# Sliding-window attention with SwiGLU and a top-2 mixture: host layouts replace the transposes of q and k

## The chip, the cores and the metric

The kernel runs on one core of a Trainium2 chip. The metric is the device time of one execution in microseconds (us). Inputs are laid out on the host before the launch, and that is not part of the time.

## The reference

Three stages follow one another. First, attention over 4 batches, 8 heads, 576 positions and 64 channels, in which a position sees itself and the 63 before it. Second, an RMS norm and a SwiGLU layer on 2304 tokens of 512, whose weights arrive as float64. Third, a noisy top-2 mixture of 8 experts.

```python
scores = scale * np.matmul(q, k.transpose(0, 1, 3, 2))
mask = (rel >= 0) & (rel < window)          # window = 64
attn = np.exp(scores - max) / (sum + 1e-09)
x = np.matmul(attn, v)                      # then (B * S, H * D)
xn = x / rms * rms_g
x = (silu(xn @ w_gate) * (xn @ w_val)) @ w_out
...
out[mask] += top2_w[mask, k, None] * (np.maximum(x[mask] @ w1[e], 0.0) @ w2[e])
```

## The kernel before

**Attention.** Work comes in 48 tasks: a task `n` is 192 positions (three windows of 64) of two heads. Task `n` belongs to group `rb = n // 4` of positions and head pair `hp = n % 4`; three groups make a batch. The functions, in the order of a task, are these. `load_qk` and `load_v` issue the DMAs on SP's queue, for two tasks at a time (index `m`), from q, k and v as they lie in memory, in runs of 64 floats. `att_t` (L199) transposes q and k on PE, four transposes into one PSUM bank (L207); DVE copies one head's q into the tile `qz` with the factor -0.125 (L213), ACT the other's (L215), and ACT copies k into `kT` (L224), a tile that holds a zero window and all 576 positions of a head pair. `qz` has two buffers and holds, for each of the three windows, a 128 by 128 block whose two diagonal quarters are the two heads and whose other quarters are zero. `att_s` (L228) multiplies them (L233, tile `sc`), adds the mask and takes the minimum on DVE (L238), takes exp on ACT (L241) and divides on POOL (L245). `att_p` transposes the result (L252, tile `pp`, ACT copy to `pT` in L254), and `att_v` multiplies with v (L268, tile `pv`, ACT copy to `xT` in L272).

**SwiGLU.** Tokens come in 6 blocks of 384 (`NB`), two groups of attention to a block. The hidden layer comes in 12 chunks of 128 (`NF`); a step `s` is one chunk of one block. `norm_a` to `norm_c` norm a block and split it into a high and a low float32r part (`xnH`, `xnL`), `m1_half` (L398, tile `gv`) and `m1_out` (L431, tile `x`) are the matmuls, three per product. The weights of a chunk `fc` are three pages (`raw`), loaded once in block 0 by `load_w` (L334); `conv_a` (ACT, L349 and L350) and `conv_b` (DVE and POOL, L361 to L364) turn float64 bits into float32, `split_w` (L369) splits them. There are 24 pages in all.

**Order.** The first eight tasks run ahead of block 0. Eight more run in each of the blocks 0 to 4, for the next block, spread over its steps by `plan_att`: the slots `at(i, ...)` are emptied between the parts of the steps. A scheduler then sets the order on each engine from this order of code. Each queue works in order. All loads named here share SP's queue. `RT`, `LG`, `AO` and their like are tables of slot numbers that don't change. The experts follow after block 5 and don't change either.

Of the kernel before, what the change touches and what calls it, by code (L numbers as in the profile page):

```python
# [23 lines left out]
def tile_window_attention_swiglu_top2(  # L24
# [139 lines left out]
    def rows(src, m, lo, ap):  # L164
        rb, hq = divmod(m, H // NH)
        b, g = divmod(rb, GS)
        o = ((b * H + NH * hq) * S + g * RG + lo) * D
        return bass.AP(tensor=src.tensor, offset=src.offset + o, ap=ap)

    qs, ks, vs, kTs, kw = {}, {}, {}, {}, {}  # L170

    def load_qk(m):
        for src, name, tiles_ in ((q, "qs", qs), (k, "ks", ks)):
            t = attn.tile([RG // 2, 2, NH, D], F32, name=f"{name}{m}", tag=name, bufs=2)
            for c in range(2):
                nc.sync.dma_start(t[:, c], rows(src, m, c * RG // 2, [[D, RG // 2], [S * D, NH], [1, D]]))
            tiles_[m] = t

    def load_v(m):
        w = attn.tile([P, 3, NH, D], F32, name=f"vw{m}", tag="vw", bufs=NVW)  # L180
        vs[m] = w
        first = (m // (H // NH)) % GS == 0
        if first:
            nc.gpsimd.memset(w[0:64, 0], 0.0)
        if m < VD:
            for i in range(3):
                nc.sync.dma_start(w[64:128, i], rows(v, m, i * WIN, [[D, WIN], [S * D, NH], [1, D]]))
            if not first:
                VE(w[0:64, 0], vs[m - H // NH][64:128, 2])
            VE(w[0:64, 1:3], w[64:128, 0:2])  # L190
            return
        if first:
            nc.sync.dma_start(w[64:128, 0], rows(v, m, 0, [[D, WIN], [S * D, NH], [1, D]]))
# [2 lines left out]
        for i in range(1, 3):
            nc.sync.dma_start(w[:, i], rows(v, m, (i - 1) * WIN, [[D, P], [S * D, NH], [1, D]]))

    def att_t(n):  # L199
        rb, hp = divmod(n, HP)  # L200
        m, u = divmod(n, 2)
        hs = slice(2 * u, 2 * u + 2)
        pt = bank(f"pt{n}")
        for i, a in enumerate((qs[m], ks[m])):
            for c in range(2):
                o = i * RG + c * RG // 2
                nc.tensor.transpose(pt[:, o:o + RG // 2], a[:, c, hs].rearrange("p h d -> p (h d)"),  # L207
                                    ident[:RG // 2, :RG // 2])
        for h in range(2):
            s = slice(64 * h, 64 * h + 64)  # L210
            sv = pt[s, :RG].rearrange("d (i c) -> d i c", c=64)
            if h == 0:
# [933 lines left out]
```

## Time and profile before

| | us |
|---|---|
| median of 3 runs | 1109.2 |
| lowest and highest of them | 1109.14, 1111.27 |
| the profiled execution | 1112.73 |
| its span in the trace | 1111.0 |
| PE busy in it | 1053.1 |
| DVE busy | 621.7 |
| ACT busy | 552.5 |
| POOL busy | 435.3 |

The span runs from the first to the last instruction of the profiled execution; its own time is 1.7 us longer, since it takes in what lies around the span. Busy time is the time in which an engine works on an instruction. Matmuls overlap, and their ends are modelled, so the distance between the starts of two PE rows tells more than their lengths. A row of the timeline is a start, a length, an engine, a line of the kernel, an operation, the tile written and the tiles read, the shape and a count (several like instructions in a row are one row), and in brackets how long the engine stood idle before and what ended that.

### The profile page before, as it was taken

Reading aid. Unit: us, or ns where it says so; the run is one execution under the profiler, and the core shown is the slowest. Engines: PE = TensorE matmul, PEld = TensorE weight load, DVE = VectorE, ACT = ScalarE, POOL = GpSimd, SP = SyncE. Lnnn points to the kernel's source line nnn. Section 1 sums busy time; section 2 is a strip of 40 time slices with the busy share of each in tenths; the row PEclk is TensorE's granted clock in tenths of the full one; section 3 lists DMA queues with packets and bytes.
Section 4 is the critical chain, followed back from the end, with each engine's and each line's share of the span. In section 5 each row is a group of like instructions: output and inputs, shape, how many; then the busy total and the mean of one; then the engine's idle time right before and its main releaser. Section 6 shows DMA issues by size and latency. Waiting matters only on the chain. (4 is left out here: it accounts for less than half of the span.)

```text
span 1111.0 us, 17699 instructions
## 1 busy us (share of the span) xinstructions
PE 1053.1 (95%) x6452; PEld 938.5 (84%) x6452; DVE 621.7 (56%) x1638; ACT 552.5 (50%) x1265; POOL 435.3 (39%) x456
## 2 busy tenths in 40 slices
PE   7688889999999999999999999999999999999993
PEld 6577778889889898988989888898989898989882
DVE  4899996766565565657576752433425343435420
ACT  6768766656565665556553522433334343433420
POOL 4366662352244225224523326334334344443211
PEclk9799999999999999999999999999999999999997
DMA  8846427111120121100020406544445445455311
GB/s 179 243 137 208 144 71 252 40 44 43 30 55 13 57 45 44 43 16 1 2 67 20 142 12 170 140 127 86 139 95 148 95 141 100 138 112 144 74 16 26
DMA packets 116408, 101.64 MB, mean 91 GB/s; under 512 B 82048, under 2 KB 94576, under 8 KB 116320
## 3 DMA queue, kind: packets, MB, share of 16 engines
q0 software_dynamic: 17904, 49.07, 18.1%
q1 hardware_dynamic: 98416, 51.42, 16.6%
q8 instruction: 52, 0.85, 0.3%
q14 instruction: 36, 0.29, 0.1%
HBM read 80.55 MB, written 19.92 MB: 90 GB/s over the span
## 5 line engine op out<-in xcount | busy, mean ns | idle before, releaser
L398 PE MATMUL gv<-xnH,gvH 128*128 128x384 f32 x576 | 203.9, 355 | 4.2 <-ACT xnH L325 3.2
L889 PE MATMUL y<-wH,hh 128*128 128x512 f32 (+1 forms) x608 | 202.3, 399 | 0.0
L398 PE MATMUL gv<-xnH,gvL 128*128 128x384 f32 x576 | 196.2, 342 | 4.3 <-DVE gvL L375 4.3
L398 PE MATMUL gv<-xnL,gvH 128*128 128x384 f32 x576 | 196.2, 341 | 0.0
L431 PE MATMUL x<-woHL,hh 128*128 128x512 f32 x648 | 174.5, 404 | 5.0 <-ACT hh L416 4.1
L384 POOL TENSOR_TENSOR woHL<-wo,woHL 128x512 fp32r<-128x512 f32 x72 | 99.3, 1380 | 147.2 <-ACT woHL L383 147.1
L431 PEld LDWEIGHTS x<-woHL,hh 128*128 128x128 f32 x648 | 119.1, 190 | 28.0 <-ACT hh L416 4.9
L889 PEld LDWEIGHTS y<-wH,hh 128*128 128x128 f32 (+1 forms) x608 | 112.9, 186 | 29.9 <-issue 1.0
L600 DVE TENSOR_TENSOR wL<-st,wH 128x1024 fp32r<-128x1024 f32 x64 | 78.3, 1227 | 100.0 <-ACT wH L599 97.9
L713 PE MATMUL h<-xpl,wH 128*128 128x272 f32 (+3 forms) x448 | 133.5, 298 | 0.2 <-issue 0.2
L713 PE MATMUL h<-xph,wH 128*128 128x272 f32 (+3 forms) x448 | 133.3, 298 | 0.0
L713 PE MATMUL h<-xph,wL 128*128 128x272 f32 (+3 forms) x448 | 133.3, 298 | 0.0
L911 POOL DMA_INDIRECT out_dram<-ys,tid x38 | 59.5, 1566 | 186.6 <-ACT ys L904 141.1
L723 DVE SCALAR_TENSOR_TENSOR hh<-h,hh 128x272 fp32r<-128x272 f32 (+6 forms) x232 | 69.6, 325 | 105.8 <-ACT hh L719 89.9
L889 PE MATMUL y<-wL,hh 128*128 128x512 f32 (+2 forms) x328 | 128.4, 395 | 0.1
L719 ACT ACTIVATE hh<-h 128x160 fp32r<-128x160 f32 (+4 forms) x184 | 61.7, 344 | 133.0 <-PE h L713 94.7
L398 PEld LDWEIGHTS gv<-xnH,gvH 128*128 128x128 f32 x576 | 109.3, 190 | 7.8 <-ACT xnH L325 4.0
L398 PEld LDWEIGHTS gv<-xnH,gvL 128*128 128x128 f32 x576 | 109.3, 190 | 6.2 <-DVE gvL L375 5.7
L398 PEld LDWEIGHTS gv<-xnL,gvH 128*128 128x128 f32 x576 | 109.4, 190 | 0.9
L375 DVE TENSOR_TENSOR gvL<-gv,gvH 128x1024 fp32r<-128x1024 f32 (+1 forms) x73 | 92.0, 1262 | 14.4 <-ACT gvH L372 12.1
L245 POOL TENSOR_TENSOR pm<-pm,st 128x384 f32<-128x384 f32 x48 | 41.1, 856 | 133.8 <-DVE st L244 97.0
L372 ACT ACTIVATE gvH<-gv 128x1024 fp32r<-128x1024 f32 x72 | 75.7, 1051 | 21.9 <-PE gv L398 15.0
(208 smaller groups left out, 1924.7 us busy)
## 6 DMA issues: line engine op xcount, KB each, us to landing
vw<-in_v_dram SPq DMA_DIRECT2D x60, 128.0 KB, 3.0
raw<-in_moe_w_gate_dram SPq DMA_DIRECT2D x12, 512.0 KB, 7.5
raw<-in_moe_w_val_dram SPq DMA_DIRECT2D x12, 512.0 KB, 4.4
raw<-in_moe_w_out_dram SPq DMA_DIRECT2D x12, 512.0 KB, 4.5
out_dram<-zero SPq DMA_DIRECT2D x1, 4864.0 KB
qs<-in_q_dram SPq DMA_DIRECT2D x48, 96.0 KB, 2.6
ks<-in_k_dram SPq DMA_DIRECT2D x48, 96.0 KB, 2.6
x2d<-xs SPq DMA_DIRECT2D x18, 256.0 KB, 2.0
```

The source lines that it names most:

```text
L245: nc.gpsimd.tensor_tensor(p, p, st[:, :, 3:4].to_broadcast([P, 3, P]), op=ALU.mult)
L372: nc.scalar.activation(h, gv[fc], AF.Copy)
L375: eng.tensor_tensor(l[:, f], gv[fc][:, f], h[:, f].bitcast(F32), op=ALU.subtract)
L384: nc.gpsimd.tensor_tensor(o[:, 512:], wo[fc], o[:, :512].bitcast(F32), op=ALU.subtract)
L398: nc.tensor.matmul(ps, a, b, start=n == 0, stop=n == 3 * KD - 1)
L431: nc.tensor.matmul(X2[j][t], a, b, start=fc == 0 and n == 0, stop=fc == NF - 1 and n == 2)
L600: nc.vector.tensor_tensor(lo, a, ho.bitcast(F32), op=ALU.subtract)
L713: nc.tensor.matmul(ps, w, x, start=i == 0, stop=i == 3 * KD - 1)
L719: nc.scalar.activation(hh[:, c0 - p0:c1 - p0], ps[:, c0 - lo:c1 - lo], AF.Relu)
L723: nc.vector.scalar_tensor_tensor(hh[:, l.start + a - s.start:l.start + b - s.start], ps[:, a + p0 - lo:b + p0 - lo], 0.0, hh[:, a:b].bitca ...
L889: nc.tensor.matmul(ps[:a.shape[1]], a, b, start=i == 0, stop=i == len(terms) - 1)
L911: nc.gpsimd.indirect_dma_start(out=out, out_offset=bass.IndirectOffsetOnAxis(ap=r[:m], axis=0), in_=y[:m], in_offset=None, compute_op=ALU. ...
```

## The change

On the host, q is laid out as one block of 128 (two heads by 64 channels) by 192 for each task, the 192 in the order position within the window, then window; k as 128 by 576 for each batch and head pair; v as positions by heads by channels, so that four heads of a position are one run of 256 floats. The float64 weights are laid out as pages of 128 by 512, as they are wanted in memory.

In the kernel `att_t` is gone. `load_q` loads each head of a task straight into its half of `qz`, which is now 128 by 2 by 192 with the other half zeroed once, in six buffers. `load_k` loads k straight into `kT`, 192 positions first and the other 384 with the second group. Both are issued four tasks ahead. The scores' stationary operand for window `i` is every third column of `qz`, from `i` on. The factor -0.125 moves into the masking instruction on DVE, and the mask's constant is scaled to suit.

```diff
+FAR = -8.0 * MASKED
...
-    NQ = 2
+    NQ = 6
...
-    qz = [attn.tile([P, 3, P], F32, name=f"qz{i}") for i in range(NQ)]
-    for t in qz:
-        nc.gpsimd.memset(t[0:64, :, 64:128], 0.0)
-        nc.gpsimd.memset(t[64:128, :, 0:64], 0.0)
+
+    qz = [attn.tile([P, 2, RG], F32, name=f"qz{i}") for i in range(NQ)]
...
+    def load_q(n):
+        rb, hp = divmod(n, HP)
+        for h in range(2):
+            d = slice(64 * h, 64 * h + 64)
+            nc.sync.dma_start(qz[n % NQ][d, h], q[rb, hp, d])
+            if n < NQ:
+                (nc.vector if n == 0 else nc.gpsimd).memset(qz[n][d, 1 - h], 0.0)
+
+    def load_k(n):
+        rb, hp = divmod(n, HP)
         b, g = divmod(rb, GS)
...
+        if g == 0:
+            kTs[hp] = attn.tile([P, WIN + S], F32, name=f"kT{n}", tag="kT", bufs=NKT)
+            nc.gpsimd.memset(kTs[hp][:, 0:WIN], 0.0)
+            nc.sync.dma_start(kTs[hp][:, WIN:WIN + RG], k[b, hp, :, 0:RG])
+        elif g == 1:
+            nc.sync.dma_start(kTs[hp][:, WIN + RG:], k[b, hp, :, RG:])
+        kw[n] = kTs[hp][:, g * RG:]
...
+        for i in range(3):
+            o = g * RG + (i - 1) * WIN
+            if o < 0:
+                nc.gpsimd.memset(w[0:64, i], 0.0)
+                nc.sync.dma_start(w[64:128, i], v[b, 0:WIN, hs, :])
             else:
-                nc.scalar.activation(qz[n % NQ][s, :, s], sv, AF.Copy, scale=-0.125)
...
+                nc.sync.dma_start(w[:, i], v[b, o:o + P, hs, :])
...
+        qzf = qz[n % NQ].rearrange("p h c -> p (h c)")
         for i in range(3):
-            nc.tensor.matmul(ps[:, i, :], qz[n % NQ][:, i, :], kt[:, i * WIN:i * WIN + P], start=True, stop=True)
+            nc.tensor.matmul(ps[:, i, :], qzf[:, bass.ds(i, P, step=3)], kt[:, i * WIN:i * WIN + P], start=True, stop=True)
...
-            nc.vector.tensor_tensor_reduce(out=p[:, i, :], in0=ps[:, i, :], in1=m, scale=1.0, scalar=MASKED,
+            nc.vector.tensor_tensor_reduce(out=p[:, i, :], in0=ps[:, i, :], in1=m, scale=-0.125, scalar=MASKED,
                                            op0=ALU.add, op1=ALU.min, accum_out=st[:, i, 0:1])
...
-            if c < 2:
-                nc.sync.dma_start(t.rearrange("p (k f) -> p k f", k=KD), srcs[c].bitcast(I32))
-            else:
-                nc.sync.dma_start(t, srcs[c].bitcast(I32))
+            nc.sync.dma_start(t, (w_gate, w_val, w_out)[c][fc].bitcast(I32))
...
-    load_qk(0)
-    load_v(0)
-    load_qk(1)
-    load_v(1)
+    for n in range(4):
+        load_k(n)
+        load_q(n)
+        if n % 2 == 0:
+            load_v(n // 2)
...
-            at(i - lag[0], att_t, n)
             at_first(i, att_s, n)
             at(i + lag[1], att_p, n)
             at(i + lag[2], att_v, n)
+            if n + 4 < NG:
+                at(i, load_k, n + 4)
+                at(i, load_q, n + 4)
             if n % 2 and n // 2 + 2 < NG // 2:
-                at(i - lag[0], load_qk, n // 2 + 2)
                 at(i - lag[0], load_v, n // 2 + 2)
```

The first place is PE at the start of the program, up to the scores of the second task. A row is a line, an operation and its tiles, the one written ahead of the arrow; the number behind the underscore tells tiles apart. Before:

```order
L207 MATMUL pt0_139<-ident_68,qs0_113 128x96
L207 MATMUL pt1_149<-ident_68,qs0_113 128x96
L207 MATMUL pt0_139<-ident_68,qs0_113 128x96
L207 MATMUL pt1_149<-ident_68,qs0_113 128x96
L207 MATMUL pt0_139<-ident_68,ks0_116 128x96
L207 MATMUL pt1_149<-ident_68,ks0_116 128x96
L207 MATMUL pt0_139<-ident_68,ks0_116 128x96
L207 MATMUL pt1_149<-ident_68,ks0_116 128x96
L233 MATMUL sc0_169<-kT0_146,qz0_107 128x128 x3
L207 MATMUL pt2_184<-ident_68,qs1_125 128x96
L233 MATMUL sc1_194<-kT1_156,qz1_108 128x128 x3
```

And in the changed program (`sc` is L204 there, `pp` L223, `pv` L239):

```order
L204 MATMUL sc0_157<-kT0_113,qz0_107 128x128 x3
L204 MATMUL sc1_177<-kT1_125,qz1_108 128x128 x3
L204 MATMUL sc2_201<-kT2_132,qz2_109 128x128 x3
L223 MATMUL pp0_216<-ident_68,pm0_161 128x128 x3
L239 MATMUL pv0_273<-pT0_220,vw0_120 64x64 x6
L204 MATMUL sc3_225<-kT3_144,qz3_110 128x128 x3
```

The transposes are gone, and the scores of three tasks stand ahead of the first `pp`.

The second place is SP's queue in block 0, around the loads of the weight chunks 2 to 5 (`raw2_0` is the first page of chunk 2). Before:

```order
L341 DMA raw2_0_579<-in_moe_w_gate_dram 128x4x256
...
L341 DMA raw3_0_642<-in_moe_w_gate_dram 128x4x256
...
L176 DMA qs6_698<-in_q_dram 96x4x64 x2
L176 DMA ks6_701<-in_k_dram 96x4x64 x2
L341 DMA raw4_0_740<-in_moe_w_gate_dram 128x4x256
L341 DMA raw4_1_742<-in_moe_w_val_dram 128x4x256
L343 DMA raw4_2_744<-in_moe_w_out_dram 128x1024
L341 DMA raw5_0_853<-in_moe_w_gate_dram 128x4x256
```

In the changed program:

```order
L177 DMA kT13_709<-in_k_dram 128x192
L167 DMA qz2_109<-in_q_dram 64x192 x2
...
L308 DMA raw2_0_521<-in_moe_w_gate_dram 128x1024
...
L308 DMA raw3_0_576<-in_moe_w_gate_dram 128x1024
...
L177 DMA kT14_816<-in_k_dram 128x192
L167 DMA qz3_110<-in_q_dram 64x192 x2
L179 DMA kT14_816<-in_k_dram 128x384
L308 DMA raw4_0_665<-in_moe_w_gate_dram 128x1024
...
L177 DMA kT15_928<-in_k_dram 128x192
L167 DMA qz4_111<-in_q_dram 64x192 x2
L179 DMA kT15_928<-in_k_dram 128x384
L308 DMA raw5_0_775<-in_moe_w_gate_dram 128x1024
```

Loads of k and q now stand directly ahead of chunks 2, 4 and 5. The buffer of `kT13` and that of `qz2` were last read by the scores of task 8, those of `kT14` and `qz3` by task 9's, those of `kT15` and `qz4` by task 10's.

## Rows read from the trace of the kernel before

**Rows 1.** Stretches: bounds, length, PE, PEld, DVE, ACT, POOL busy, clock, DMA share, GB/s.
```profile
0.00:40.35 40.35, 26.74 (x227) 22.86 (x227) 20.92 (x110) 25.13 (x88) 15.47 (x67) 0.95 0.85 197
40.35:150.00 109.65, 91.53 (x540) 78.44 (x541) 103.27 (x190) 85.45 (x195) 72.49 (x63) 0.93 0.58 176
150.00:169.80 19.80, 18.43 (x106) 17.18 (x105) 18.89 (x35) 11.08 (x25) 10.03 (x9) 1.00 0.03 3
...
267.30:364.90 97.60, 97.28 (x635) 88.16 (x634) 60.12 (x193) 57.50 (x145) 35.16 (x36) 1.00 0.16 40
...
561.90:636.20 74.30, 73.93 (x395) 67.28 (x393) 50.63 (x111) 34.28 (x55) 22.69 (x18) 1.00 0.26 79
```
**Rows 2.** Timeline of ACT at the end of block 0.
```profile
169.81 0.58 ACT L442 ACTIVATE xs<-x 128x512 f32<-128x512 f32 x1
```
**Rows 3.** Timeline of PE in block 3, four transposes between gv matmuls.
```profile
366.62 0.34 PE L398 MATMUL gv<-xnH,gvL 128*128 128x384 f32 x1
366.80 0.33 PE L207 MATMUL pt<-ident,qs 96*128 96x96 f32 x2
...
367.07 0.42 PE L398 MATMUL gv<-xnH,gvH 128*128 128x384 f32 x1
367.33 0.34 PE L398 MATMUL gv<-xnL,gvH 128*128 128x384 f32 x1
```
**Rows 4.** Timeline of PE in block 2, four transposes behind pv.
```profile
306.29 0.38 PE L207 MATMUL pt<-ident,qs 96*128 96x96 f32 x2
...
306.62 0.42 PE L398 MATMUL gv<-xnH,gvH 128*128 128x384 f32 x1
306.87 0.34 PE L398 MATMUL gv<-xnL,gvH 128*128 128x384 f32 x1
```
**Rows 5.** Groups by line: busy us, mean ns, idle before; L213 of 40.35 to 169.8.
```profile
L213 DVE TENSOR_SCALAR qz<-pt 64x192 f32<-64x192 f32 x9 | 3.1, 342 | 0.0
...
L215 ACT ACTIVATE qz<-pt 64x192 f32<-64x192 f32 x48 | 15.7, 327 | 31.4 <-DVE qz L213 25.5 <-DVE st L243 3.1 <-DVE pi L549 2.3
...
L349 ACT ACTIVATE raw<-raw 128x512 f32<-128x512 f32 x36 | 24.4, 678 | 0.0
...
L383 ACT ACTIVATE woHL<-wo 128x512 fp32r<-128x512 f32 x72 | 45.4, 630 | 57.0 <-PE gv L398 31.2 <-PE x L431 15.0 <-DVE wo L364 6.1
```
**Rows 6.** Timeline of PE's weight loads, the scores of one task.
```profile
284.40 0.75 PEld L233 LDWEIGHTS sc<-kT,qz 128*128 128x128 f32 x6
```
**Rows 7.** Timeline of SP's DMA queue.
```profile
0.75 0.92 SPq L176 DMA_DIRECT2D qs<-in_q_dram  x2
...
20.91 0.51 SPq L341 DMA_DIRECT2D raw<-in_moe_w_gate_dram  x1
...
61.45 0.37 SPq L341 DMA_DIRECT2D raw<-in_moe_w_gate_dram  x1
...
81.88 1.05 SPq L197 DMA_DIRECT2D vw<-in_v_dram  x2
```
**Rows 8.** DMA issues by tile: count, size, median us from issue to landing.
```profile
raw<-in_moe_w_val_dram SPq DMA_DIRECT2D x12, 512.0 KB, 4.4
...
qs<-in_q_dram SPq DMA_DIRECT2D x48, 96.0 KB, 2.6
```
**Rows 9.** Timeline of PE: scores of tasks 0 and 7, first gv matmul.
```profile
6.61 1.62 PE L233 MATMUL sc<-kT,qz 128*128 128x128 f32 x6 [1.04 <-ACT kT L224]
...
24.74 0.94 PE L233 MATMUL sc<-kT,qz 128*128 128x128 f32 x6 [0.31 <-ACT kT L224]
...
40.35 0.69 PE L398 MATMUL gv<-xnH,gvH 128*128 128x384 f32 x1 [1.32 <-ACT xnH L325]
```
**Rows 10.** Timeline: task 10's scores, its last exp, then chunk 5's first page.
```profile
75.51 0.94 PE L233 MATMUL sc<-kT,qz 128*128 128x128 f32 x6 [2.20 <-ACT kT L224]
...
78.45 0.19 ACT L241 ACTIVATION_READ_ACCUMULATOR pm<-pm,st 128x1 f32 x1
...
81.37 0.67 ACT L349 ACTIVATE raw<-raw 128x512 f32<-128x512 f32 x1
```

More of the change, by code (lines that the diff above doesn't have):

```diff
@@ L42, in tile_window_attention_swiglu_top2 @@
     P = 128
-    B, H, S, D = q.shape
+    B, S, H, D = v.shape
     N, E = noise.shape
@@ L46, in tile_window_attention_swiglu_top2 @@
     KD = DM // P
-    FF = w_gate.shape[1]
-    NF = FF // P
+    NF = w_gate.shape[0]
     F2 = w1.shape[2]
@@ L104, in tile_window_attention_swiglu_top2 @@
         lo = float(-64 * h)
-        nc.vector.tensor_scalar(mask[s], rel[s], lo, MASKED, op0=ALU.is_le, op1=ALU.mult)
-        nc.vector.tensor_scalar(scr[s], rel[s], lo + 64.0, MASKED, op0=ALU.is_gt, op1=ALU.mult)
+        nc.vector.tensor_scalar(mask[s], rel[s], lo, FAR, op0=ALU.is_le, op1=ALU.mult)
+        nc.vector.tensor_scalar(scr[s], rel[s], lo + 64.0, FAR, op0=ALU.is_gt, op1=ALU.mult)
     nc.vector.tensor_tensor(mask, mask, scr, op=ALU.add)
     nc.vector.tensor_copy(mask0, mask)
-    nc.vector.memset(mask0[:, 0:64], MASKED)
+    nc.vector.memset(mask0[:, 0:64], FAR)
     nc.vector.tensor_tensor(fold, ident[:4 * E, 0:2 * E], ident[:4 * E, 2 * E:4 * E], op=ALU.add)
@@ L127, in tile_window_attention_swiglu_top2 @@
     GS = S // RG
-    NQ = 2
+    NQ = 6
     NVW = 4
-    VD = 2
-    VE = nc.gpsimd.tensor_copy
     CA, LA = 0, 2
@@ L162, in tile_window_attention_swiglu_top2 @@
     NH = 4
-    def rows(src, m, lo, ap):
-        rb, hq = divmod(m, H // NH)
-        b, g = divmod(rb, GS)
[L167 to L177, printed above, removed]
+    vs, kTs, kw = {}, {}, {}
+    def load_q(n):
[7 more added lines that the diff above has]
+        rb, hp = divmod(n, HP)
+        b, g = divmod(rb, GS)
+        if g == 0:
[5 more added lines that the diff above has]
+        kw[n] = kTs[hp][:, g * RG:]
     def load_v(m):
@@ L181, in load_v @@
         vs[m] = w
[L182 to L193, printed above, removed]
-        else:
-            nc.sync.dma_start(w[:, 0], rows(v, m, -WIN, [[D, P], [S * D, NH], [1, D]]))
@@ L196, in load_v @@
[L196 to L212, printed above, removed]
-                nc.vector.tensor_scalar(qz[n % NQ][s, :, s], sv, -0.125, None, op0=ALU.mult)
-            else:
-                nc.scalar.activation(qz[n % NQ][s, :, s], sv, AF.Copy, scale=-0.125)
-        if rb % GS == 0:
-            kTs[hp] = attn.tile([P, WIN + S], F32, name=f"kT{n}", tag="kT", bufs=NKT)
-            nc.gpsimd.memset(kTs[hp][:, 0:WIN], 0.0)
-        kt = kTs[hp][:, rb % GS * RG:]
-        kw[n] = kt
-        if n in KD_:
-            nc.vector.tensor_copy(kt[:, WIN:WIN + RG], pt[:, RG:2 * RG])
-        else:
-            nc.scalar.activation(kt[:, WIN:WIN + RG], pt[:, RG:2 * RG], AF.Copy)
@@ L226, in tile_window_attention_swiglu_top2 @@
+        rb, hq = divmod(m, H // NH)
+        b, g = divmod(rb, GS)
+        hs = slice(NH * hq, NH * hq + NH)
+        for i in range(3):
[3 more added lines that the diff above has]
+                nc.sync.dma_start(w[64:128, i], v[b, 0:WIN, hs, :])
+            else:
+                nc.sync.dma_start(w[:, i], v[b, o:o + P, hs, :])
     Pm, PT = {}, {}
@@ L334, in load_w @@
     def load_w(fc, cs=(0, 1, 2)):
-        fs = slice(fc * P, fc * P + P)
-        srcs = (w_gate[:, fs].rearrange("(k p) f -> p k f", p=P), w_val[:, fs].rearrange("(k p) f -> p k f", p=P),
-                w_out[fs, :])
         for c in cs:
             t = page(I32, f"raw{fc}_{c}")
-            if c < 2:
-                nc.sync.dma_start(t.rearrange("p (k f) -> p k f", k=KD), srcs[c].bitcast(I32))
-            else:
-                nc.sync.dma_start(t, srcs[c].bitcast(I32))
+            nc.sync.dma_start(t, (w_gate, w_val, w_out)[c][fc].bitcast(I32))
             RAW[fc, c] = t.rearrange("p (n w) -> p n w", w=2)
@@ L1134 @@
         a = _np.ascontiguousarray(inputs[name])
+        if name == "q":
+            B, H, S, D = a.shape
+            a = a.reshape(B, H // 2, 2, S // 192, 3, 64, D).transpose(0, 3, 1, 2, 6, 5, 4)
+            a = _np.ascontiguousarray(a).reshape(B * S // 192, H // 2, 128, 192)
+        elif name == "k":
+            B, H, S, D = a.shape
+            a = _np.ascontiguousarray(a.transpose(0, 1, 3, 2)).reshape(B, H // 2, 2 * D, S)
+        elif name == "v":
+            a = _np.ascontiguousarray(a.transpose(0, 2, 1, 3))
         if a.dtype == _np.float64:
+            if name != "moe_w_out":
+                a = a.reshape(4, 128, -1, 128).transpose(2, 1, 0, 3)
+            a = _np.ascontiguousarray(a.reshape(-1, 128, 512))
             a = a.view(_np.int64)
```

## The prediction

> **What bounds the kernel now.** I read the busy time by stretch first, then the two sides of the largest stretch, then the queue that starts the loads.
>
> [rows 1] cut the span at the ends of the blocks, which are the moments at which ACT copies a block's result out of PSUM ([rows 2] is block 0's). Three kinds of stretch show. From 0 to 40.35 us no engine is full: the first eight attention tasks run as a chain, and the DMA engines are 85% busy. From 40.35 to 169.8 us (block 0) DVE works 103.27 + 18.89 = 122.2 of 129.45 us, 94%, while PE has gaps: DVE turns twelve float64 weight chunks into float32 there, and it sets the pace. From 169.8 to 561.9 us (blocks 1 to 4) PE is busy more than 99.5% of each block at the full clock (1.00), so each PE instruction taken out shortens the block by what it took. Block 5 has no attention and lasts 74.3 us where block 2 lasts 97.6. What follows after 636.2 us is not touched.
>
> **The change part by part.** The program order shows that the 192 transposes of q and k (L207) are gone, with 96 ACT copies (L215, L224) and 48 DVE copies (L213), and that 32 DMAs are added on SP's queue.
>
> *Blocks 1 to 4, transposes.* In [rows 3] four transposes stand alone between two gv matmuls: from 366.80 to 367.07 is 0.27 us, and the gv matmul behind them needs 0.26 us to the next where 0.18 is usual (the rows of one stream are 0.17 to 0.18 apart), so a group alone costs 0.27 + 0.08 = 0.35. In [rows 4] they follow the pv matmuls: 306.29 to 306.62 is 0.33, and the slow step behind them stays, since pv would cause it. Of the 32 groups in these blocks 18 stand behind pv and 14 alone: 18 x 0.33 + 14 x 0.35 = 10.8 us. PE has no other cover there, so **-10.8**. The ACT and DVE copies of these blocks lie beside PE work and give nothing: DVE is busy 62% there.
>
> *The strided stationary operand.* The score matmuls now load every third float32 of a row. The six records of a task's scores load in 0.75 us [rows 6]; a load lasts about 0.19, so one follows another every (0.75 - 0.19) / 5 = 0.11 us, and half of that, 0.055, I count as the load, since both halves move 128 columns. No row shows a stationary operand with a step. From below the price is 0. From above I take twice the load: 32 tasks x 6 x 0.055 = 10.6 us; a gain from a step is excluded, as no fewer elements are read. The nearest row is ACT's: reading every second 32-bit word, 512 of them, takes 678 ns (L349), reading 512 in a row 630 (L383) [rows 5], 8% more. A wider step and a faster reader suggest more: I take 20%, 0.011 x 192 = **+2.1**.
> [...]
>
> *Block 0.* DVE loses nine qz copies of 342 ns [rows 5]: since DVE is the bound, **-3.1**. The 16 ACT copies of 0.33 us lie in ACT's idle time (85.45 busy of 109.65 us). Against this stands a new order on SP. SP issues in order, and the weight chunks now stand behind loads of k and q whose buffers a score matmul must free first: raw2 waits behind kT13 and qz2 for the scores of task 8, raw5 behind kT15 and qz4 for those of task 10. Bound for one chunk: below 0; above, after that matmul four DMAs of 0.5 us each [rows 7] must be issued before the chunk's first page leaves, and the page lands 4.4 us later [rows 8], 6.4 us behind the scores. Before, task 10's scores began at 75.51 and its exps were over at 78.64, from where ACT could go on to the pages [rows 10], 3.1 us; so a chunk comes up to 3.3 us late. The order puts four chunks (2, 5, 10, 11) as tight as that: 0 to 13.2 us. ACT idles a fifth of the time and DVE queues other work, which covers most of it; I take one whole wait, chunk 2's, the first and least covered: **+3.3**.
>
> *The start.* The scores of task 0 no longer wait for transposes, copies and kT: before they began at 6.61 [rows 9]. Now they need three DMAs instead of four, the third issued at 0.75 + 2 x 0.52 = 1.8 us and landed 2.6 us later [rows 7, 8]: 4.4. But this lead is not kept whole, because SP issues one DMA every 0.52 us (the last two of a v load take 1.05 [rows 7]). The q of task 7 is the 36th issue: 0.75 + 35 x 0.52 = 19.0, landed at 21.6; the scores of task 7 began at 24.74 before [rows 9]. That is 3.1 us. ACT, which every task crosses, loses 2 x 0.33 of some 3.2 us per task, and the sum-of-squares step moves ahead of two weight conversions on DVE; I add 1.4 for these. The first weight chunk is the 41st issue now and was the 37th: it leaves at about 21.6 instead of 20.91 [rows 7]; with 4 KB runs for 1 KB it should land no later. So the first gv matmul moves from 40.35 to about 35.9: **-4.5**, with 0 (the later weight pages hold it) and -8 (ACT's whole 8 x 0.66 and the rest of the lead) as ends.
>
> *At no price.* The score scale moves into the masking instruction, which has the same shape; the memsets of the six q tiles run on POOL and DVE beside the first loads, which end later. The v loads keep their number.
>
> Sum: -10.8 + 2.1 - 3.1 + 3.3 - 4.5 = -13.0 us. The profiled execution took 1112.73 us, 3.5 above the median of the runs; against its own time the sum gives 1099.7, against the median of 1109.2 it gives **1096**. A measurement of this kernel tells about 0.2% (2.2 us) from no change.
>
> **Rivals.**
> A. *The start gives nothing.* The eight tasks finish earlier, but chunk 2's pages leave only after task 8's scores, and DVE, the bound from there on, stands until they land. For it: 41 issues before the first weight page, one more DMA ahead of each chunk. Against: DVE still has chunk 1 to convert and split at that point. Time: 1096 + 4.5 = 1100.7.
> B. *The strided load takes twice as long.* Place: PE in blocks 1 to 4, where nothing hides it. 10.6 instead of 2.1: 1104.7. For: a step of two costs ACT something already [rows 5], and PE reads faster than ACT. Against: that it is only 8%. The break-even point is a load 0.055 + (13.0 + 2.1) / 192 = 0.13 us long. [...]
> C. *Slower: weight chunks starve block 0.* One mechanism: SP's in-order queue holds each of chunks 2 to 11 behind a k, q or v load that waits for attention, and attention waits for DVE, which waits for the chunk. Price 3.3 us per chunk, less ACT's idle fifth: 10 x 3.3 x 0.78 = 26 us in place of 3.3, so 1118.7. It decides from (13.0 + 3.3) / 10 = 1.6 us per chunk that nothing covers. For: SP's order above. Against: before the change a chunk left long before its use (chunk 5 issued at 61.45, converted at 81.37 [rows 7, 10]), and most chunks still pass a task ahead.
> D. *All goes well*: the start gives 8, strides and pages cost nothing: 1109.2 - 10.8 - 3.1 - 8 = 1087.3.
> That the change doesn't do what it says is excluded by the program order.
>
> **How the numbers follow.** Forecast 0.52, A 0.16, B 0.13, C 0.09, D 0.10. The range runs from a little below D, 1085, to A and B together (1096.2 + 4.5 + 8.5 = 1109.2), of which I keep 1108; outside lie C and the far ends. C alone, with a little of A and B combined, gives slower 0.09; within 0.2% lie A and B together, 0.04; faster is the rest, 0.87.
>
> **What would show it.** Right: block ends 97.5 us apart shrink to 94 to 96; the first gv matmul starts at 35 to 37 us; the six score loads of a task stay under 0.8 us; few runs of 256 bytes are left among the DMA packets. Wrong: score loads spaced at 0.15 us or more (B); ACT's page conversions waiting for DMA in block 0, or the block longer than 129.45 us (A, C).

## The result and the profile after

The changed kernel takes 1123.2 us (median of 4 runs, 1122.36 to 1123.95) against 1110.2 for the kernel before in the same session: a ratio of 1.0115, with a 95% interval of 1.0097 to 1.0133. It is slower by 13 us; the prediction said 1096 and faster.

The windows view of the profile after, cut as [rows 1] was, at its own block ends (columns as there: busy us of each engine with counts, PE's granted clock, DMA share, GB/s):

```profile
0.00:39.06 39.06, 24.01 (x195) 20.52 (x196) 17.03 (x102) 20.26 (x72) 15.89 (x71) 0.92 0.69 206
39.06:150.00 110.94, 87.93 (x489) 76.87 (x490) 100.19 (x180) 76.42 (x172) 65.06 (x57) 0.87 0.54 178
150.00:181.57 31.57, 25.54 (x122) 22.85 (x122) 21.91 (x38) 15.11 (x30) 16.82 (x14) 0.89 0.08 23
279.87:377.76 97.89, 97.39 (x602) 88.24 (x601) 59.09 (x183) 52.17 (x128) 35.11 (x36) 1.00 0.12 35
573.20:647.31 74.11, 73.97 (x395) 67.26 (x393) 49.85 (x111) 34.35 (x55) 23.35 (x18) 1.00 0.26 79
```

Block 0 lasts from 39.06 to 181.57, 142.5 us, where it was 129.45 [rows 1]. Block 2 lasts 97.9 where it was 97.6, though its transposes are gone; it is still full of PE work at the full clock. Block 5 has not moved. The timeline of ACT and PE after has the marks that answer to [rows 2] and [rows 9]:

```profile
4.16 1.62 PE L204 MATMUL sc<-kT,qz 128*128 128x128 f32 x6 [4.16 <-DMA qz<-in_q_dram]
...
24.87 1.41 PE L204 MATMUL sc<-kT,qz 128*128 128x128 f32 x6
...
39.06 1.01 PE L363 MATMUL gv<-xnH,gvH 128*128 128x384 f32 x2 [1.32 <-ACT xnH L296]
...
181.57 0.58 ACT L407 ACTIVATE xs<-x 128x512 f32<-128x512 f32 x1
```

Task 0's scores come 2.5 us sooner, task 7's not at all, the first gv matmul 1.3 us sooner. So the two spans, 1111.0 and 1120.5, differ by -1.3 (start) + 13.1 (block 0) - 0.5 (blocks 1 to 4: 391.6 for 392.1) - 0.2 (block 5) - 1.6 (the rest) = +9.5. The medians differ by 13.0, since the profiled execution of before (1112.73) was 2.5 us above the median of 1110.2 and that of the changed kernel (1122.36) 0.9 below its own.

Three things are to be explained: where the transposes' gain went, what makes block 0 longer, and why the start gave so little.

### The profile page after: what moved, and what is told of

Same layout as the page of the kernel before. It is cut to its first block, busy times and chain, and to the rows that moved or that the text cites. A ratio compares the mean times of both kernels' runs of the same rounds, so it can differ in the third digit from the quotient of the medians.

```text
span 1120.5 us, 17203 instructions
## 1 busy us (share of the span) xinstructions
PE 1053.4 (94%) x6260; PEld 940.9 (84%) x6260; DVE 610.5 (54%) x1592; ACT 522.4 (47%) x1169; POOL 437.1 (39%) x460
## 3 DMA queue, kind: packets, MB, share of 16 engines
HBM read 80.81 MB, written 19.92 MB: 90 GB/s over the span
## 5 line engine op out<-in xcount | busy, mean ns | idle before, releaser
L363 PE MATMUL gv<-xnH,gvH 128*128 128x384 f32 x576 | 203.9, 357 | 14.1 <-ACT gvH L337 12.8
L396 PE MATMUL x<-woHL,hh 128*128 128x512 f32 x648 | 177.4, 406 | 10.1 <-ACT hh L381 9.9
L396 PEld LDWEIGHTS x<-woHL,hh 128*128 128x128 f32 x648 | 119.0, 191 | 32.2 <-ACT hh L381 10.8
L340 DVE TENSOR_TENSOR gvL<-gv,gvH 128x1024 fp32r<-128x1024 f32 (+1 forms) x73 | 88.3, 1210 | 27.7 <-ACT gvH L337 18.2
```

The costliest lines, as they stand in the source:

```text
L340: eng.tensor_tensor(l[:, f], gv[fc][:, f], h[:, f].bitcast(F32), op=ALU.subtract)
L363: nc.tensor.matmul(ps, a, b, start=n == 0, stop=n == 3 * KD - 1)
L396: nc.tensor.matmul(X2[j][t], a, b, start=fc == 0 and n == 0, stop=fc == NF - 1 and n == 2)
```

## The experiments

The table has what each run gave: the median, the ratio to the kernel before in the same session with its interval, and from the trace the first gv matmul (the beginning of block 0), the length of block 0, of blocks 1 to 4 together, and the time from the first gv matmul to ACT's first conversion of weight chunk 2, which will matter. E8 is a program of its own and has no row.

| run | median us | ratio | first gv | block 0 | blocks 1-4 | chunk 2 at |
|---|---|---|---|---|---|---|
| before | 1108.1 to 1110.2 | | 40.4 | 129.5 | 392.1 | +6.9 |
| after | 1123.2 | 1.0115 [1.0097, 1.0133] | 39.1 | 142.5 | 391.6 | +12.7 |
| E1 | 1111.0 | 1.0025 [1.0012, 1.0038] | 39.3 | 141.9 | 381.5 | +14.8 |
| E2 | 1119.8 | 1.0104 [1.0087, 1.0122] | 39.9 | 129.2 | 402.9 | +6.9 |
| E3 | 1109.1 | 1.0010 [1.0001, 1.0020] | 38.3 | 129.6 | 391.8 | +7.4 |
| E4 | 1107.5 | 0.9998 [0.9987, 1.0009] | 38.3 | 130.3 | 390.7 | +8.4 |
| E5 | 1100.2 | 0.9928 [0.9915, 0.9941] | 39.1 | 132.6 | 380.6 | +9.2 |
| E6 | 1093.7 | 0.9858 [0.9843, 0.9873] | 34.8 | 130.1 | 380.5 | +7.4 |
| E7 | 1117.1 | 1.0073 [1.0058, 1.0088] | 39.2 | 138.5 | 392.0 | +11.8 |
| E9 | 1112.5 | 1.0037 [1.0024, 1.0050] | 43.3 | 130.1 | 390.7 | +8.5 |
| E10 | 1094.5 | 0.9867 [0.9853, 0.9882] | 36.5 | 130.2 | 380.7 | +8.9 |
| E11 | 1101.6 | 0.9937 [0.9923, 0.9951] | 38.5 | 132.6 | 380.6 | +9.2 |
| E12 | 1100.4 | 0.9926 [0.9913, 0.9940] | 41.8 | 129.1 | 380.6 | +7.3 |
| E13 | 1107.0 | 0.9984 [0.9975, 0.9994] | 38.9 | 130.0 | 390.8 | +12.3 |
| E14 | 1107.6 | 0.9990 [0.9981, 1.0000] | 38.5 | 129.8 | 390.7 | +12.3 |
| E15 | 1109.0 | 1.0004 [0.9993, 1.0014] | 37.6 | 129.6 | 390.7 | +13.2 |
| E16 | 1110.0 | 1.0012 [1.0002, 1.0021] | 38.7 | 132.6 | 390.7 | +14.1 |
| E17 | 1122.6 | 1.0134 [1.0116, 1.0151] | 37.9 | 143.8 | 391.7 | +14.7 |
| E18 | 1109.0 | 1.0009 [0.9999, 1.0018] | 38.0 | 131.5 | 391.1 | +9.6 |

### The step of three: E1, E2, E8

E1 undoes the step alone, in the changed kernel:

```diff
-    qz = [attn.tile([P, 2, RG], F32, ...
+    qz = [attn.tile([P, 3, P], F32, ...
...
-            nc.sync.dma_start(qz[n % NQ][d, h], q[rb, hp, d])
+            nc.sync.dma_start(qz[n % NQ][d, :, d], q[rb, hp, d].rearrange("d (i c) -> d i c", i=3))
...
-            nc.tensor.matmul(ps[:, i, :], qzf[:, bass.ds(i, P, step=3)], kt...
+            nc.tensor.matmul(ps[:, i, :], qz[n % NQ][:, i, :], kt...
```

> The changed kernel with q kept as [128, 3, 128] with zero quarters, so that the score matmuls load 128 neighbouring float32 again; q arrives in runs of 256 bytes. Nothing else, and the order on PE, DVE, ACT and SP is the changed kernel's. Theory (the step costs some 0.07 us per load): score loads back from 0.27 to 0.20 us, blocks 1 to 4 from 391.6 to about 378 us, block 0 only a few us shorter, time 1123.2 - 13.5 - 0 to 3 = 1107 to 1110. Rival (the blocks lost their gain to something else, such as waits for q and k): blocks stay within 2 us of 391.6 and the time at 1121 or more.

Blocks 1 to 4 went from 391.6 to 381.5 us, 10.1 less; block 0 stayed (141.9). E2 adds the step alone, to the kernel before:

```diff
-            nc.vector.tensor_scalar(qz[n % NQ][s, :, s], sv, -0.125, None, op0=ALU.mult)
+            nc.vector.tensor_scalar(qz[n % NQ][s, h].rearrange("d (c i) -> d i c", i=3), sv, -0.125, None, op0=ALU.mult)
...
+            nc.tensor.matmul(ps[:, i, :], qzf[:, bass.ds(i, P, step=3)], kt...
```

> The kernel before, with its transposes, but its copies put q so that the stationary operand of the scores takes every third float32; nothing else, same order on every engine. Theory (0.07 us per load): blocks 1 to 4 grow from 392.1 to about 405.5 us, time 1110.2 + 13.5 = 1123.7, up to 1127 if block 0 pays for its 48 loads too. Rival (the loads are longer but PE covers them): time within 2 us of 1110.2.

Blocks 1 to 4 grew by 10.8 us, block 0 not at all. So the theory holds and the rival falls: 10.1 to 10.8 us over 192 loads is 0.053 to 0.056 us for each. The size expected, 13.5, was too large: it came from the lengths of the load records, and those overlap: the six of a task, of 0.19 us each, lie within 0.75 [rows 6]. The timeline of the loads, summed from 200 to 500 us (minimum, median and maximum in ns), first of the changed kernel, then of E1:

```profile
L204 PEld LDWEIGHTS sc<-kT,qz x146: 251/261/263, 206.8 to 500.0; 128*128 128x128 f32 x146
```

```profile
L203 PEld LDWEIGHTS sc<-kT,qz x150: 187/192/192, 205.7 to 491.7; 128*128 128x128 f32 x150
```

A record is 69 ns longer with the step; the lengths of the blocks show 53 to 56 of them. E8 measures the step by itself, in a program that does none of the task's work and was run once:

```diff
+    for i in range(48):
+        nc.tensor.matmul(dst(i), w[:, bass.ds(0, P, step=3)], m[:, 0:P], start=True, stop=True)
```

> Not the task's work: series of 48 float32 score-like matmuls (128x128 stationary, 128 moving columns, two passes each) one behind the other, with the stationary operand at steps of 1, 2, 3, 4, 6 and 8 elements, then the moving operand at steps of 2, 3 and 4, then the same stationary steps in bfloat16; all of it twice. Theory (a load at step 3 takes 0.053 us longer, from E1): step 3 adds some 0.05 us per load. [...] Rival: the load grows with the step itself, 2 already costs, 8 most.

The groups by line of E8's first half: stationary steps 1, 2, 3, 4, 6 and 8 in float32 (L43 to L53), moving steps 3 and 4 (L57, L59), stationary steps 1 and 4 in bfloat16 (L61, L67).

```profile
L53 PE MATMUL ps<-m,w 128*128 128x128 f32 x96 | 23.0, 401 | 0.0
...
L49 PE MATMUL ps<-m,w 128*128 128x128 f32 x96 | 22.6, 397 | 0.0
L59 PE MATMUL ps<-m,w 128*128 128x128 f32 x96 | 21.9, 405 | 0.0
...
L51 PE MATMUL ps<-m,w 128*128 128x128 f32 x96 | 21.7, 387 | 0.0
L47 PE MATMUL ps<-m,w 128*128 128x128 f32 x96 | 16.8, 337 | 0.0
...
L57 PE MATMUL ps<-m,w 128*128 128x128 f32 x96 | 16.8, 344 | 0.0
...
L45 PE MATMUL ps<-m,w 128*128 128x128 f32 x96 | 11.5, 281 | 0.0
...
L43 PE MATMUL ps<-m,w 128*128 128x128 f32 x96 | 10.9, 275 | 0.0
L61 PE MATMUL ps<-mb,wb 128*128 128x128 bf16 x48 | 2.9, 219 | 0.0
...
L67 PE MATMUL ps<-mb,wb 128*128 128x128 bf16 x48 | 2.8, 219 | 0.0
```

The busy time of a series divided by its 96 records is the pace of a load with its matmul: 0.114 us at step 1, 0.120 at step 2, 0.175 at step 3, 0.235 at step 4 and 0.226 to 0.240 beyond. With half of 0.114 taken as the plain load, an estimate, a load takes twice as long at step 3 and three times at step 4 and above; step 2 costs 0.006 us. The moving operand comes to nearly the same, 0.175 us at step 3 and 0.228 at step 4; a bfloat16 stationary operand takes 0.060 at step 1 and 0.058 at step 4. So the 0.05 us expected at step 3 came as 0.061, and the rival's growth with the step ends at step 4: 0.235, 0.226 and 0.240 at steps 4, 6 and 8.

### The parts of the change, and the first theory of block 0: E3, E4, E5, E7

E3 takes the page layout alone into the kernel before (the new `load_w` and the host's layout of float64 pages).

> The kernel before with the float64 pages alone laid out in large pieces; same order on every engine. Theory (page layout gives nothing, block 0 is set by conversions): 1110 +- 2 us, block 0 127 to 131 us. Rival (pages that land sooner shorten block 0, or delay it by crowding other loads): 1106 or less, or 1114 or more.

Block 0 129.6 us, time the same within the 0.2% that can be told: the pages give nothing and cost nothing.

The changed kernel's trace shows ACT waiting 4.12 us for chunk 2's first page at 51.73 (its row is shown further down) and PE standing 7.01 us for the split behind it:

```profile
53.92 0.69 PE L363 MATMUL gv<-xnH,gvH 128*128 128x384 f32 x1 [7.01 <-ACT gvH L337]
```

So the first theory was rival C in one chunk: chunk 2 leaves SP's queue late. E4 moves it ahead:

```diff
+    def behind(f, *a):
+        with tc.issue_after(RI[2]):
+            f(*a)
...
-                at(i, load_k, n + 4)
-                at(i, load_q, n + 4)
+                for f in (load_k, load_q):
+                    at(i, *((behind,) if n + 4 in range(12, 20) else ()), f, n + 4)
```

(`RI[2]` is the last load of chunk 2; v's loads are treated alike.)

> The changed kernel with weight chunk 2 issued before the k, q and v loads of tasks 12 to 19, so that it no longer stands behind the scores of tasks 8 and 9. Theory (block 0 is long because weight chunks start late behind those loads): chunk 2 issues at about 40 us instead of 46.3, ACT's wait of 4.1 us and PE's stall of 7.0 us at 54 us go, block 0 from 142.5 to about 135 us, time 1123.2 - 7 = 1116. Rival (chunk 2 lies beside other work that is late anyway; block 0 is long for another reason): block 0 stays above 140 us, time 1121 to 1125.

Block 0 fell by 12 us to 130.3, more than the theory wanted, which should have been a warning. E5 puts E1's and E4's edits together.

> E1 and E4 together: q contiguous for the score loads, and chunk 2 ahead of the loads of tasks 12 to 19. Theory (two separate losses, the step in blocks 1 to 4 and the late chunk in block 0): 1107.5 - 10.1 = 1097.4, between 1096 and 1099; blocks 1 to 4 at 381 us, block 0 at 128 to 131 us. Rival (E4 gained by a luckier order of instructions, which the two edits together lose again): block 0 over 135 us, time 1102 or more.

1100.2, 1.2 above the range: blocks 1 to 4 as expected, block 0 2.3 us longer than E4's. E7 tries the reverse on the kernel before:

```diff
+            if fc == 2 and c == 0:
+                a = srcs[0].bitcast(I32)
+                for r in range(2):
+                    b = dram.tile([P, KD, 256], I32, name=f"bounce{r}")
+                    nc.sync.dma_start(b, a)
+                    a = b
+                nc.sync.dma_start(t.rearrange("p (k f) -> p k f", k=KD), a)
```

> The kernel before, whose first page of weight chunk 2 takes a way round over two copies in DRAM, so that it lands some 5 us later; little else in the order moves. Theory (a chunk 2 that lands late shifts ACT's in-order work and with it block 0): ACT waits 3 to 5 us for the page, block 0 grows by 6 to 12 us, time 1114 to 1120. Rival (lateness alone is absorbed, and block 0 of the changed kernel is long by its order of instructions): block 0 grows by 3 us or less, time 1108 to 1111.

Block 0 grew by 9.1 us. By then nothing in E1 to E7 spoke against a late chunk 2. But ACT did not wait 3 to 5 us for the page in E7 as expected (0.82 us for that page; its longest wait for a page, 2.23 us, is at 147.15, near the end of the block), and both E4 and E7 had also changed the order of instructions on ACT, DVE and PE: the scheduler orders every engine anew when a load moves.

### Lateness or order: E9, E13 to E18

E9 loads k and q two tasks ahead:

```diff
-            if n + 4 < NG:
-                at(i, load_k, n + 4)
-                at(i, load_q, n + 4)
+            if 4 <= n + 2 < NG:
+                at(i, load_k, n + 2)
+                at(i, load_q, n + 2)
```

> The changed kernel with k and q loaded two tasks ahead instead of four (step 3 kept). Weight chunks 0 and 1 leave earlier, but chunk 2 still stands behind tasks 12 to 14, whose q waits for the scores of task 8; the order on PE, DVE and ACT comes nearer to E4's than to the changed kernel's. Theory (a late chunk 2 costs block 0 its 9 to 12 us whatever the order): chunk 2 issues after 44 us, block 0 stays at 138 us or more, time 1117 to 1123. Rival (the order of the changed kernel does it, lateness only in part): block 0 at 130 to 134 us, time 1108 to 1112.

Chunk 2 left at 48.0 us, later than in the changed kernel (46.3), yet block 0 took 130.1. That was not clean, as the block itself began 4.2 us later. E13, E14 and E15 are to delay the landing: E4 with chunk 2's first page read from a spread-out copy in short runs of 256, 128 and 64 bytes. The order moves with it, since the scheduler counts the delay.

```diff
+            if (fc, c) == (2, 0):
+                src = w_gate[NF:NF + 2].bitcast(I32).rearrange("a p (n t w) -> (a p n) t w", t=2, w=64)[:, 0]
+                src = src.rearrange("(p n) w -> p n w", p=P)
```

> E4 with the first page of chunk 2 read in 2048 runs of 256 bytes instead of 128 of 4 KB, so that it lands later. Theory (lateness counts once it passes a slack of some 5 us behind the first gv matmul): lands 2 to 6 us later than in E4, still within the slack, block 0 130 to 134 us, time 1107 to 1111. Rival (any disturbance of the order costs 10 us): block 0 over 136 us.

> E13 with runs of 128 bytes (4096 of them) for that page; the same order on every engine as E13. Theory (lateness): the page lands some 4 to 10 us later than in E13, and block 0 is longer by that much or up to twice that, less what is left of the slack: 4 to 15 us over E13. Rival (the order sets block 0): block 0 within 2 us of E13's.

> E14 with runs of 64 bytes (8192), nearly the same order. Theory (lateness): as much again later as E14 to E13, block 0 longer by one to two us for each us of lateness. Rival (order): block 0 within 3 us of E13's.

Chunk 2 was converted 12.3 to 13.2 us behind the first gv matmul, as late as in the changed kernel (12.7), and block 0 took 129.6 to 130.0 us. So a late conversion by itself costs nothing. But the page was not as late as its conversion: in E15 it landed at 47.06, 12.2 us behind the start of its issue at 34.88, the changed kernel's at 51.7, 5.4 behind its own at 46.27, and ACT, which had the split `gvH` and `hh` ahead of it, came to it at 50.89 without a wait. (E13 and E14 were meant as two doses in one order, but both met ACT at the same +12.3, so they tell nothing of a dose.)

E16 and E17 do the same to the changed kernel, whose loads keep their places: with runs of 256 bytes the scheduler counts the delay and writes another order, with runs of 512 bytes every engine keeps the changed kernel's.

> The changed kernel, loads where they were, with the first page of chunk 2 read in runs of 256 bytes: chunk 2 later still, and the scheduler, which counts that, writes another order on ACT, DVE and PE (153 rows of PE's 5006 differ). Theory (the order makes block 0 long: in-order queues put late work ahead of work that others wait for): block 0 at 129 to 135 us although chunk 2 is converted later than in the changed kernel, time 1109 to 1115. Rival (a late chunk 2): block 0 at 142 us or more, time 1122 to 1128.

> The changed kernel, with the first page of chunk 2 read in runs of 512 bytes; the order on every engine is the changed kernel's. Theory (order): block 0 stays at 141 to 146 us, time 1122 to 1126. Rival (lateness): the same and longer by one to two us for each us that the page lands later; below 138 us neither holds.

Chunk 2 is converted 14.1 and 14.7 us behind the first gv matmul, nearly alike, and here the page itself is late: ACT waits for it in both; block 0 takes 132.6 us in the one and 143.8 in the other, and the times are 1110.0 and 1122.6. The same loads, the same lateness, another order: 11 us. Here is the place where the two first part. The timeline of ACT in the changed kernel, in E17 (its order) and in E16:

```profile
51.73 0.65 ACT L314 ACTIVATE raw<-raw 128x512 f32<-128x512 f32 x1 [4.12 <-DMA raw<-in_moe_w_gate_dram]
...
52.83 1.04 ACT L337 ACTIVATE gvH<-gv 128x1024 fp32r<-128x1024 f32 x1
...
61.23 0.41 ACT L212 ACTIVATE pm<-pm,st 128x128 f32<-128x128 f32 x1 [3.77 <-DVE st L209]
...
66.71 0.46 ACT L372 ACTIVATE th<-gv 128x384 f32<-128x384 f32 x1
```

```profile
52.66 0.65 ACT L320 ACTIVATE raw<-raw 128x512 f32<-128x512 f32 x1 [6.00 <-DMA raw<-in_moe_w_gate_dram]
...
53.76 1.04 ACT L343 ACTIVATE gvH<-gv 128x1024 fp32r<-128x1024 f32 x1
...
62.15 0.40 ACT L212 ACTIVATE pm<-pm,st 128x128 f32<-128x128 f32 x1 [3.77 <-DVE st L209]
...
67.69 0.46 ACT L378 ACTIVATE th<-gv 128x384 f32<-128x384 f32 x1
```

```profile
50.05 1.06 ACT L343 ACTIVATE gvH<-gv 128x1024 fp32r<-128x1024 f32 x1 [2.01 <-DVE gv L335]
...
51.53 0.51 ACT L387 ACTIVATE hh<-th 128x384 fp32r<-128x384 f32 x1
...
52.79 0.68 ACT L320 ACTIVATE raw<-raw 128x512 f32<-128x512 f32 x1 [0.75 <-DMA raw<-in_moe_w_gate_dram]
...
58.98 0.46 ACT L378 ACTIVATE th<-gv 128x384 f32<-128x384 f32 x1
```

In the changed kernel ACT's queue has chunk 2's conversion ahead of the split `gvH` of chunk 1, which PE's next step needs: ACT waits for the page with work behind it that does not need the page. In E16 the split and `hh` come first and the page is waited for 0.75 us. The second step's tanh then comes at 58.98 instead of 66.71, since in the changed kernel the next exps, which wait for DVE, and two more conversions and a split stand ahead of it. The wait table of PE in block 0, its two largest waits in the changed kernel and the same two in E16 (us in total, times, longest):

```profile
PE gv L363 <- ACT gvH L337: 12.8, 3, 7.0
PE x L396 <- ACT hh L381: 9.9, 3, 6.6
```

```profile
PE x L402 <- ACT hh L387: 6.1, 2, 4.3
PE gv L369 <- ACT gvH L343: 5.0, 3, 3.8
```

In total, 22.7 us of waiting for ACT became 11.1, while the wait for POOL's `pm` grew from 4.3 to 9.5. The windows view of block 0 as a whole, E17 then E16:

```profile
37.90:181.70 143.80, 111.60 (x609) 97.75 (x610) 122.52 (x217) 91.68 (x202) 81.65 (x71) 0.90 0.45 146
```

```profile
38.70:171.30 132.60, 110.14 (x612) 96.98 (x613) 119.04 (x218) 92.39 (x203) 79.09 (x71) 0.94 0.49 156
```

DVE, the engine that sets the pace of the block, stands idle for 21.3 us in E17, 20.4 in the changed kernel, 13.6 in E16, and stood idle for 7.3 in the kernel before [rows 1]. So of the 11.2 us between E17 and E16 7.7 are idle time of DVE and 3.5 are longer instructions. Most of that difference in idle time stands behind ACT's split; in the groups by line of the two blocks, E17 then E16 (the last field is idle time before the group):

```profile
L346 DVE TENSOR_TENSOR gvL<-gv,gvH 128x512 fp32r<-128x512 f32 (+1 forms) x15 | 14.4, 963 | 9.3 <-ACT gvH L343 9.3
```

```profile
L346 DVE TENSOR_TENSOR gvL<-gv,gvH 128x512 fp32r<-128x512 f32 (+1 forms) x15 | 15.5, 1038 | 2.5 <-ACT gvH L343 2.3
```

Lateness has its share in the first stall. In E4 ACT's order is the changed kernel's up to this split, the page is in time, and PE's wait for the split is 4.61 us; it is 7.01 in the changed kernel and 8.89 in E17, where the page is later. PE's rows in E4 and E17:

```profile
50.78 0.69 PE L367 MATMUL gv<-xnH,gvH 128*128 128x384 f32 x1 [4.61 <-ACT gvH L341]
```

```profile
54.85 0.69 PE L369 MATMUL gv<-xnH,gvH 128*128 128x384 f32 x1 [8.89 <-ACT gvH L343]
```

The block does not follow: E1 has the changed kernel's order and a wait of 8.84, and its block 0 is 141.9 for 142.5. What the changed kernel's whole order costs with the page in time was not run.

PE's granted clock in block 0 is 0.90 in E17 and 0.94 in E16, and 0.90 too in E6, whose block 0 is 130.1 us long; what it adds was not measured.

E18 has such a late page in the kernel before with its new pages.

> E3 (the kernel before with the page layout) with the first page of chunk 2 in runs of 256 bytes, so late that the scheduler writes another order. Theory (order): block 0 anywhere from 129 to 139 us, not tied to when chunk 2 is converted. Rival (lateness): block 0 as in E7 by chunk 2's time, 130 + (start of its conversion behind the first gv matmul - 7) us or more.

Block 0 131.5 us with chunk 2 at +9.6: lateness wanted 132.6 or more, so this run tells little by itself.

What stays open is which exchange of places costs how much. The tanh of the second step comes 7.7 us later in the changed kernel than in E16, that of the fourth 2.2 (79.44 and 77.27), that of the eighth 12.0 (130.03 and 118.06): the first stall is mostly caught up, and the rest is lost anew at later places (PE's 6.6 us at 121.9, behind `hh` on ACT; ACT's waits for pages at 147.24 and 151.08, 3.4 us together). No order was written by hand to try one exchange alone. E7's 9.1 us are in the same state: order and lateness moved together, and after E13 to E17 order is the likelier cause.

### The start: E6, E10, E11, E12

E6 is E5 with q's tiles written whole by the host, zeros included:

```diff
-        for h in range(2):
-            d = slice(64 * h, 64 * h + 64)
-            nc.sync.dma_start(qz[n % NQ][d, h], q[rb, hp, d])
-            if n < NQ:
-                (nc.vector if n == 0 else nc.gpsimd).memset(qz[n][d, 1 - h], 0.0)
+        nc.sync.dma_start(qz[n % NQ], q[rb, hp])
```

> As E5, but the host writes q with its zero quarters, so that a task's q is one DMA of 128 x 1536 bytes: 48 DMAs fewer on SP's queue, no memsets of q on POOL, twice the bytes of q. Theory (SP's issues at 0.58 us per q DMA and POOL's memsets hold the start): scores of task 7 and the first weight page 5 to 7 us earlier, first gv matmul at 33 to 36 us, time 1092 to 1095. Rival (the first eight tasks are held by their own chain over DVE, ACT and PE, or by bytes): first gv matmul still at 38 to 40 us, time 1096 to 1099.

1093.7 us. The scores of task 7 begin at 19.0, the first weight page leaves at 18.76 and the first gv matmul starts at 34.81, 5.5 us sooner than before. The timeline of SP's queue in the changed kernel, then of SP and PE in E6:

```profile
1.21 1.20 SPq L167 DMA_DIRECT2D qz<-in_q_dram  x2
...
19.92 1.95 SPq L167 DMA_DIRECT2D qz<-in_q_dram  x2
...
23.97 0.50 SPq L308 DMA_DIRECT2D raw<-in_moe_w_gate_dram  x1
```

```profile
1.22 0.42 SPq L165 DMA_DIRECT2D qz<-in_q_dram  x1
...
18.76 0.50 SPq L307 DMA_DIRECT2D raw<-in_moe_w_gate_dram  x1
...
19.01 0.83 PE L199 MATMUL sc<-kT,qz 128*128 128x128 f32 x6
...
34.81 1.01 PE L362 MATMUL gv<-xnH,gvH 128*128 128x384 f32 x2 [1.26 <-ACT xnH L291]
```

The two half tiles of 64 partitions take SP 1.1 to 1.2 us to issue together (tasks 0 to 6), 0.55 to 0.60 each; the whole tile, with four times the bytes of a half, takes 0.42 at 1.22. E6 has eight issues fewer ahead of the first weight page. In the first 40 us of the changed kernel PE waits for q's loads (us in total, times, longest):

```profile
PE sc L204 <- DMA qz<-in_q_dram: 7.6, 3, 4.2
```

E11 tells the memsets from the issues, on E5:

```diff
-                (nc.vector if n == 0 else nc.gpsimd).memset(qz[n][d, :, 64 - 64 * h:128 - 64 * h], 0.0)
+                nc.vector.memset(qz[n][d, :, 64 - 64 * h:128 - 64 * h], 0.0)
```

> E5 with the zero quarters of the q tiles written by DVE instead of POOL, ahead of the masks; two q DMAs per task as in E5. Theory (SP's issues hold the start): first gv matmul stays within 1 us of E5's 39.1, time 1099 to 1101. Rival (POOL's memsets, for which the first scores wait 4 us, hold it): first gv matmul at 37 us or earlier, time 1096 to 1098.

38.5 against 39.1: taking the memsets from POOL to DVE is worth 0.6 us of the 4.3 between E5 and E6. The rest goes with q's DMAs, fewer and whole; E6 has a new order on the engines too, whose share was not told apart. E10 is E6 without E4's edit.

> E6 without the move of chunk 2: q in whole tiles with its zeros, chunk 2 behind the loads of tasks 12 to 14 again. Theory (late chunk 2): the queue is shorter by 13 issues at that place, so chunk 2 leaves some 4 to 6 us later than in E6, and block 0 is 4 to 10 us longer than E6's 130.1: time 1098 to 1104. Rival (chunk 2's place does not matter once the queue is short): block 0 within 2 us of 130, time 1093 to 1096.

Chunk 2's first page lands 8 us later than in E6 (45.4 and 37.1) and block 0 is the same, 130.2 us; E4's edit is not needed. E12 loads two tasks ahead in E6, as E9 did.

> E6 with k and q loaded two tasks ahead: the first weight pages pass four tasks' loads, and fewer loads wait for buffers. Theory (after E6 the first weight chunk and the attention chain both still wait for SP's queue): first weight page 2 to 4 us earlier, first gv matmul at 32 to 34 us, time 1090 to 1093. Rival (the chain of the eight tasks and the sum of squares sets the first gv matmul by now): 34.8 us and 1093 to 1095, or later scores and a longer start, up to 1098.

The first weight page left 5.7 us sooner, at 13.1, but the first gv matmul came 7 us later, at 41.8: the rival had a longer start among its cases, though not one as long (1098 at most for 1100.4). Loads two ahead cost the eight tasks of the start more than the weights gain, in E9 (43.3) as here (task 7's scores at 25.3 for 19.0); four ahead is better.

E6 and E10 beat both kernels, by 1.4% and 1.3% against before: what the change gains, without the step, and with one DMA for each q tile.

## Why the prediction was wrong

**Transposes, -10.8: right.** E1 against before, blocks 1 to 4: 381.5 for 392.1, -10.6.

**The strided stationary operand, +2.1: the size failed.** The runs give +10.1 and +10.8, the upper bound of 10.6 and the price of rival B. The step that failed is "the nearest row is ACT's (...) 8% more. A wider step and a faster reader suggest more: I take 20%". That row was good for a step of two, where E8 has 11% more for the load (0.063 for 0.057), but the cost turns between two and three (0.120 and 0.175 us with the matmul in E8), and nothing in it could show that. So the transposes' gain was given back in full, and blocks 1 to 4 show -0.5.

**Block 0, -3.1 + 3.3: failed by 13 us.** I priced chunk 2's lateness and SP's queue, and took the order on ACT, DVE and PE for that of before less what was gone. That is the step: "Against this stands a new order on SP". The new order was on all engines. Rival C had the place and the sign (1118.7 for 1123.2), but its mechanism only in part: ACT does wait for pages, 8.1 us in the block, but with a page as late in another order (E16) the block takes 132.6 us. The -3.1 did not show either: the nine copies are gone, and DVE's busy time in the block is 122.10 for 122.17. With the same instructions it was 119.0 in E16 and 122.5 in E17, so the lengths of DVE's instructions are not fixed. In the groups by line of block 0, before and after, for one:

```profile
L364 DVE SCALAR_TENSOR_TENSOR gv<-raw 128x512 int32<-128x512 int32 x22 | 17.8, 828 | 0.1
```

```profile
L329 DVE SCALAR_TENSOR_TENSOR gv<-raw 128x512 int32<-128x512 int32 x22 | 22.5, 1038 | 0.1
```

The record shows what goes with it. In before, after, E16 and E17 each of these conversions that has no POOL instruction beside it takes 0.67 to 0.69 us, and each one over 0.8 has one beside it. Over 0.8 are 6 before, 12 after, 8 in E16 and 12 in E17. One of each kind, from the timelines of DVE and POOL after and of E16:

```profile
57.12 1.48 POOL L349 TENSOR_TENSOR woHL<-wo,woHL 128x512 fp32r<-128x512 f32 x1
57.36 1.78 DVE L329 SCALAR_TENSOR_TENSOR gv<-raw 128x512 int32<-128x512 int32 x1
```

```profile
59.28 0.69 DVE L335 SCALAR_TENSOR_TENSOR gv<-raw 128x512 int32<-128x512 int32 x1
```

An instruction beside it does not always lengthen it: at 133.57 in the changed kernel the conversion takes 0.68 us, all but 0.02 of it beside POOL's 1.81 from 133.59. No run kept POOL away from them, so that POOL is the cause is the author's estimate and was not shown.

**The start, -4.5: came to -1.3.** The step that failed is "SP issues one DMA every 0.52 us". Up to task 7's q, the 35th and 36th issue, it was one every (19.92 - 0.75) / 34 = 0.56 us, as it had been before ((20.91 - 0.75) / 36 by [rows 7]); this pair took 1.95 us and was out at 21.87, where 19.5 was forecast. So the scores of task 7 began at 24.87 instead of 21.6, and the first weight page left at 23.97, 2.4 us later than the 21.6 I gave it. The 3.1 us of lead is what was lost. The 1.4 us for ACT and the sum of squares came, untested: from task 7's scores to the first gv matmul it was 15.6 us before and 14.2 after. With one DMA a tile (E6) the start gives 5.5.

**At no price: nearly held.** Page layout (E3); the memsets had 0.6 us (E11); the packets under 512 bytes fell as foretold, from 82048 to 11904.

**The signs named beforehand.** Block ends 97.9 apart instead of 94 to 96, a task's six score loads at 1.12 to 1.18 us in blocks 1 to 4 instead of under 0.8, block 0 over 129.45 and ACT waiting for a page: each pointed to B or to the place of C, and all could be read off the trace before a run. The range reached to A and B together, 1108; B and C together were never added. That C's number alone lies 5 us from the result is luck: it has block 0 some 23 us longer, where 13.1 came, and the strided load still at 2.1.

## What to carry to other kernels

A free layout is free only if its reader can read it: give the stationary operand of float32 matmuls neighbouring elements or a step of two (0.114 and 0.120 us with the matmul in E8, 0.175 at step 3, which the moving operand takes at step 3 too), and let the host write the zeros if that makes one whole-tile DMA of several small ones (0.42 us of SP's time in E6 for 1.1 to 1.2). When loads move under a scheduler, compare the order on every engine around the first waits before pricing anything, above all which work in an in-order queue stands behind work that waits. An edit that fixes a wait and also moves the order proves nothing about the wait; delay the same data in the same order, or keep the delay and change the order.
